# Early rows of an expert listed from 72 instead of 80 columns, their weights split on VectorE, later keys moved into the expert stage, five lists undeferred

## The chip, the cores and the metric

The kernel runs on one core of a Trainium2 chip. The metric is the device time of one execution in microseconds. One execution of each kernel was also profiled; times inside it are counted from the start of its span.

## The reference

Two layers follow each other. The first is a gated recurrence over 4 sequences of 5056 tokens with 256 channels; the second sends each of the 20224 rows to one of 8 experts with a capacity of 2528 rows each, by a greedy order over all (row, expert) logits, and runs that expert's two-layer network.

```
sig = 1 / (1 + exp(-f_logit)); f = lb + (1 - lb) * sig
for t in range(S): h = f[:, t] * h + (1 - f[:, t]) * x[:, t]; y[:, t] = h
logits = y.reshape(N, D) @ w_gate                 # N = 20224, D = 256, E = 8
for idx in argsort(-logits.flatten()):            # best pair first
    tok, e = idx // E, idx % E
    if assigned[tok] >= 0 or counts[e] >= N // E: continue
    assigned[tok] = e; counts[e] += 1
for e in range(E): out[assigned == e] = relu(y[assigned == e] @ w1[e]) @ w2[e]   # F = 1024
```

## The kernel before

Rows are held as 158 columns of 128 rows (a column is a tile of rows, NT = 158).

**Stage 1, the recurrence.** A loop over 40 chunks of four columns loads `x` and `f_logit` with SyncE's queue, takes the sigmoid on ScalarE, multiplies on GpSimd, transposes on TensorE, scans on VectorE (`g`) and transposes back with the logits beside the rows (`back`, PSUM `pr`, result `hr`). The rows go to a DRAM buffer `hbuf` from a ring of 22 buffers, half of them while the loop still loads and the rest behind it. `prep(c0, c1)` makes the keys of a block of columns in six steps: the best logit (`M`), its expert (`TMP`, `A`), an integer key (`K`), a one-hot table (`O`) and the first level of masks (`MK`). The loop does blocks of 32 columns as they become ready, and the last ones behind its end.

**Early rows.** When the keys of the first `CE` columns are there, `early` picks an expert that has at least `EARLY` first choices there (the fewest of those), loads its weights (`first_weights`, raw tiles `r`) and lists its first `EARLY` rows (`ids`), spread over the loop's iterations. `further` lists `MORE` rows from the remaining columns. These rows make a slot of their own, slot -1, of 14 tiles of 128 rows. `cut` notes which rows were taken (`EM`).

**Routing.** `route(r)` for r = 0 to 7 finds, round by round, the expert that fills first and the threshold of its last row. `search` does two halves of four levels: masks on VectorE (`MK`, two instructions of 80 columns), 20 small matmuls (`rt`), a masked sum (`DM`, `CR`), a matmul, a comparison (`FL`), a matmul and a new threshold (`TH`). At its end `GP` gives the result, then `assign`, `update`. `compact` writes the list of a slot, groups of two or three tiles at a time (`ids`), with sums on ScalarE (`junk`); a list starts only when the list ahead of it is done (`free`). For rounds below `AHEAD` the list of slot r follows round r at once; from `AHEAD` on a slot's list is made one round later (`pick`, `note`), so that the early rows' expert can be left to the last slot.

**Stage 2, the experts.** Slots -1 to 7 are worked through in chunks of up to four tiles, eight steps each. A step is `first` (six matmuls into `pw`, ScalarE writes `hh`, VectorE `hl`) and, three steps later, `second` (matmuls into `py` with both halves of `w2`). Operands are split into a high and a low part: `split` makes `w1h`, `w2s` on ScalarE and the low parts `w1l`, `w2s` on VectorE. For slot -1 two of the four low parts of w1 and all of w2 are made on GpSimd. Rows come by indirect DMAs of GpSimd (`gather`, tile `xg`) and are transposed (`trans`, `pt`, `xh`, `xl`).

**Order.** TensorE, VectorE and ScalarE run in the order in which the program issues. The program issues the expert steps and, at each `tick`, background generators: the routing (`main`), lists (`comp`) and weights (`sp`). A planner (`Pace`) with costs per instruction decides whether an engine would be free soon enough; `tick(True)` and `until` force a step whatever it says. When the gather of a slot's first chunk comes up, `ids_of` forces the routing and the list until its ids exist. While slot -1 runs, the routing pauses as long as slot 0 has fewer than eight tiles of ids. Before the first expert step the program forces a tick of the routing beside each piece of the first weights:

```
    sp = Bg(split(-1))
    main.tick(True)
    while not have(-1, "w1"):
        sp.tick(True)
        main.tick(True)
    trans(-1, 0, 0, True)
    main.tick(True)
    trans(-1, 0, 1, True)
```

Of the kernel before, what the change touches and what calls it, by code (L numbers as in the profile page):

```python
# [106 lines left out]
def kernel(ctx: ExitStack, tc: tile.TileContext, x: bass.AP, f_logit: bass.AP,  # L107
# [28 lines left out]
    CE, EARLY, MORE, AHEAD = 80, 1024, 768, 3  # L136
# [9 lines left out]
    PS, LASTC = 2, 152  # L146
# [190 lines left out]
    RSE = state.tile([P, CE + 2], BF, name="RSE")  # L337
    RAE = state.tile([P, CE + 2], BF, name="RAE")
    lv.tensor_copy(RSE[:, CE:CE + 1], pv)
    lv.tensor_copy(RSE[:, CE + 1:], pv)  # L340
# [198 lines left out]
    def blocks(ps, b0, n, w, at, ids):  # L539
        p3 = ps[:, :n * w].rearrange("p (b w) -> p b w", w=w)  # L540
        r = ohp.tile([P, 3, 4], F32, name="r")
        v.tensor_tensor(r[:, 0, :n], sq[:, b0:b0 + n], p3[:, :, w - 2], op=OP.subtract)
        v.tensor_scalar(r[:, 2, :n], p3[:, :, w - 1], float(at), None, op0=OP.add)
        yield
        for b in range(n):
            junk = ohp.tile([P, CE], F32, name="junk2")
# [3 lines left out]
        v.scalar_tensor_tensor(ids, r[:, 1, :n], float(P), r[:, 2, :n], op0=OP.mult, op1=OP.add)  # L550

    def ranks(c0, c1):
        em = EM[:, c0:c1]
        v.tensor_scalar(em, A1[:, c0:c1], ecode, 0.0, op0=OP.is_equal, op1=OP.add, accum_out=ecnt)
        v.tensor_tensor_scan(RSE[:, CE - c1 + c0:CE], onec[:, c0:c1], em, 0.0, op0=OP.mult, op1=OP.add)

    def offsets(ps, w):
        nc.tensor.matmul(ps[:, 160:161], tri, ecnt, start=True, stop=True)
        nc.tensor.matmul(ps[:, :w], nsub, RSE[:, CE + 2 - w:], start=True, stop=True)

    def steps_of(ps, w, rows):
        v.tensor_copy(RAE[:, :w], ps[:, :w])
        v.tensor_tensor(RAE[:, w - 2:w - 1], ecnt, RAE[:, w - 3:w - 2], op=OP.subtract)
        v.tensor_scalar(elim, ps[:, 160:161], -1.0, float(rows), op0=OP.mult, op1=OP.add)

    def cut(c0, c1):
        em = EM[:, c0:c1]
        v.scalar_tensor_tensor(em, RSE[:, CE - c1 + c0:CE], elim, em, op0=OP.is_le, op1=OP.mult)
        v.tensor_scalar(em, em, ecode, None, op0=OP.mult)

    def early(wi, ids):

        with nc.allow_low_precision(reason=EXACT):
            v.tensor_reduce(CR, O[:, :CE].rearrange("p c e -> p e c"), AX.X, OP.add)
        yield 'PE'
        ps = ppr.tile([P, 512], F32, name="pr")
        nc.tensor.matmul(ps[:, :E], ones_r, CR, start=True, stop=True)
        yield 'DVE'
        v.tensor_scalar(Q8, ps[:, :E], float(EARLY), 1.0e6, op0=OP.is_lt, op1=OP.mult)
        v.tensor_tensor(Q8, Q8, ps[:, :E], op=OP.add)  # L580
# [12 lines left out]
        g1 = {}  # L593
        st = ohp.tile([P, len(groups)], F32, name="st")

        def ge(k):
            g1[k] = ohp.tile([P, 512], BF, name="g1")
            v.tensor_scalar(g1[k], IO, st[:, k:k + 1], None, op0=OP.is_ge)
        v.tensor_scalar(st[:, 0:1], ps[:, 160:161], 0.0, None, op0=OP.add)
        v.tensor_scalar(st[:, 1:2], ps[:, 160:161], -512.0, None, op0=OP.add)  # L600
        steps_of(ps, w, EARLY)
        yield 'DVE'
        ge(0)
        for k in range(2):
            yield 'PE'
            ps = ppr.tile([P, 512], F32, name="pr")
            for b in range(4):
                nc.tensor.matmul(ps[:, b * w:(b + 1) * w], g1[k][:, b * P:(b + 1) * P], RAE, start=(b == 0),
                                 stop=(b == 3), skip_group_check=True)
            yield 'DVE'  # L610
            for n, _ in enumerate(blocks(ps, 4 * k, 4, w, 0, ids[:, 4 * k:4 * k + 4])):
                if n % 2:
                    yield 'DVE'
            if k == 0:
                yield 'DVE'
                ge(1)
        yield 'DVE'
        cut(0, CE)

    def further(rt, ids, prog):  # L620

        ranks(CE, NT)
        w = NT - CE + 2
        yield 'PE', RSE, ecnt
        ps = rt.tile([P, 512], F32, name="rt")
        offsets(ps, w)
        yield 'DVE', ps
        st = ohp.tile([P, len(groups)], F32, name="st")
        g1 = {}

        def ge(k):
            g1[k] = ohp.tile([P, 512], BF, name="g1")
            v.tensor_scalar(g1[k][:, :384], IO[:, :384], st[:, k:k + 1], None, op0=OP.is_ge)
        for k in range(2):
            v.tensor_scalar(st[:, k:k + 1], ps[:, 160:161], -384.0 * k, None, op0=OP.add)
        steps_of(ps, w, MORE)
        ge(0)
        for k in range(2):
            yield 'PE', RAE, g1[k]
            ps = rt.tile([P, 512], F32, name="rt")  # L640
            for b in range(3):
                nc.tensor.matmul(ps[:, b * w:(b + 1) * w], g1[k][:, b * P:(b + 1) * P], RAE[:, :w], start=(b == 0),
                                 stop=(b == 2), skip_group_check=True)
            yield 'DVE', ps
            if k == 0:
                ge(1)
            for _ in blocks(ps, 3 * k, 3, w, CE * P, ids[:, EARLY // P + 3 * k:EARLY // P + 3 * k + 3]):
                yield 'DVE',
            prog["ids"] = EARLY // P + 3 * k + 3
        cut(CE, NT)  # L650
        yield 'DVE',

# [73 lines left out]
    def prep(c0, c1):  # L726
# [3 lines left out]
        far = nc.vector if c1 > 128 else nc.gpsimd  # L730
# [46 lines left out]
    for i in range(NCH + 1):  # L777
# [7 lines left out]
        if i >= 1:  # L785
            back(i - 1)
            while stored < min(i - 1, int(SR * (i - 1)), CE // KT - 2):
                store(stored)
                stored += 1
        if i >= 4:  # L790
            build(2)
        upto = chunks[i - 1][0] // 8 * 8 if i else 0
        upto = NC if i == NCH else min(upto, LASTC)
        if upto - done >= 32 or upto > done and upto in (CE, LASTC, NC):
            preps.append(prep(done, upto))
            done = upto
        prep_step(99 if i == NCH else (3 if upto == CE else 1 if est is not None else PS) if upto < LASTC else 5)
        if due == 'PE':
            next(est)
        elif est is None and done >= CE and not preps:  # L800
            est = early(WIE, IDE)
    for _ in est:
        pass
# [94 lines left out]
def moe(ctx, tc, g):  # L898
# [8 lines left out]
    tri, cM, IO, RA, sq, ident = (g[k] for k in ("tri", "cM", "IO", "RA", "sq", "ident"))  # L907
# [19 lines left out]
    def layout(k):  # L927
        ns = {-1: [4, 4, 4, 2], E - 1: [4, 2]}.get(k, [4] * 5)
# [43 lines left out]
    def split(k):  # L972
# [61 lines left out]
    posts, step = [], 0  # L1034
# [63 lines left out]
    def second(k, c, j):  # L1098
# [3 lines left out]
        for q, n in enumerate(ns):  # L1102
# [17 lines left out]
            elif j == FB - 1 and q % 2 == 1:  # L1120
                turn = (len(SC) + sum(what[0] == "s" for what, _ in issues)) // 2
                issue(upto=lambda what: what[0] == "s" and what[1] <= turn - YB)
                y = yp.tile([P, 2, D], F32, name="y")
                m = min(ns[q - 1:q + 1])
                if m == P:
                    nc.scalar.activation(y, PY[q // 2], AF.Copy)
                else:
                    nc.scalar.activation(y[:, 0], PY[q // 2][:, 0], AF.Copy)
                    nc.scalar.activation(y[:n, 1], py, AF.Copy)
                issues.extend((("s", turn), store(k, c, r, ns[r], y)) for r in (q - 1, q))  # L1130
# [37 lines left out]
    def all_routes():  # L1168
# [3 lines left out]
        def slot(k):  # L1172
# [8 lines left out]
            return WI[k], spawn  # L1181
        for r in range(E):
            yield from route(r, rt, slot, free)

# [14 lines left out]
    comp[-1] = Bg(further(rc, IDS[-1], prog[-1]))  # L1199
    gather(*order[0])  # L1200
    issue(4)
    sp = Bg(split(-1))
    main.tick(True)
    while not have(-1, "w1"):
        sp.tick(True)
        main.tick(True)
    trans(-1, 0, 0, True)
    main.tick(True)
    trans(-1, 0, 1, True)
    gather(*gathers.pop(0))  # L1210
    issue(4)
    while not sp.done:
        sp.tick(True)
        main.tick(True)
    sp = None
# [4 lines left out]
    def tick():  # L1220
# [9 lines left out]
        if sp is None:  # L1230
# [134 lines left out]
```

## Time and profile before

| what | value |
|---|---|
| median of 3 runs | 1226.45 us (1224.43 to 1227.23) |
| the profiled execution's own time | 1225.41 us |
| its span | 1223.5 us |
| TensorE matmul busy | 1157.2 us, 95% |
| VectorE busy | 810.8 us, 66% |
| ScalarE busy | 538.2 us, 44% |
| GpSimd busy | 473.6 us, 39% |
| mean granted TensorE clock | 0.977 |

PE is TensorE's matmuls, PEld its weight loads, DVE VectorE, ACT ScalarE, POOL GpSimd, SP SyncE. PEclk is the granted TensorE clock as a share of its full speed. Matmuls overlap, so busy time of TensorE is not its peak rate. The chain from the recurrence to the expert stage is the part of the profile around 160 to 200 us; the eight large slots follow from about 288 us.

### The profile page before, as it was taken

What the parts mean: (1) busy time and instruction counts of PE and PEld (TensorE: products, weight loads), DVE (VectorE), ACT (ScalarE), POOL (GpSimd) and SP (SyncE); (2) the same over time, 40 slices, a digit from 0 to 9 for tenths busy, and PEclk for the clock granted to TensorE, in tenths of its full rate; (3) what the DMA queues carried; (4) which work ended last, traced back from release to release, by engine and by line L of the source; (5) the groups of instructions that cost most, each with busy time, mean ns of one, the idle gap of its engine ahead of it and who ended that gap; (6) DMA issues with size and microseconds to landing.
All of it is one profiled execution on the core that took longest, in us unless ns stands there. A gap on an engine that the chain in (4) does not pass through costs nothing.

```text
span 1223.5 us, 22589 instructions
## 1 busy us (share of the span) xinstructions
PE 1157.2 (95%) x8821; PEld 1050.9 (86%) x8821; DVE 810.8 (66%) x1945; ACT 538.2 (44%) x1088; POOL 473.6 (39%) x468
## 2 busy tenths in 40 slices
PE   7999767999999999999996899999999999999997
PEld 7898756889889888999895788889899899999996
DVE  6999897678778767778777678867644542252221
ACT  7887662254335425342223434443544642352332
POOL 6666672333334333333222244234333333433322
PEclk9999987999999999999997999999999999999999
DMA  9998994121131113111102113013111311211100
GB/s 357 352 337 301 342 337 140 40 100 53 45 103 54 45 47 104 48 41 40 43 27 92 36 48 108 31 44 122 44 45 52 109 44 48 98 63 48 43 31 31
DMA packets 52447, 125.25 MB, mean 102 GB/s; under 512 B 8062, under 2 KB 28288, under 8 KB 51184
## 3 DMA queue, kind: packets, MB, share of 16 engines
q0 software_dynamic: 19248, 60.96, 15.0%
q1 hardware_dynamic: 32544, 62.78, 14.8%
q8 instruction: 71, 1.16, 0.4%
q14 instruction: 40, 0.33, 0.1%
q10 hardware_dynamic: 544, 0.01, 0.0%
HBM read 81.69 MB, written 42.10 MB: 101 GB/s over the span
## 4 chain that ended last, share of the span: by engine, by line
PE 56%; issue 19%; POOL 9%; DVE 3%; ACT 1%; DMA 1%; POOLq 0%; ACTq 0%; DVEq 0%
PE py L100 25%; PE pw L100 24%; POOL out_dram L100 4%; POOL xg L100 4%; PE rt L100 3%; PE pt L100 1%; PE pr L100 1%; DMA xg<-hbuf,ids 1%; POOL r L100 1%; DVE MK L100 1%; DVE TMP L100 0%; PE pf L100 0%; PE pb L100 0%; ACT w1h L100 0%; DVE K L100 0%
## 5 line engine op out<-in xcount | busy, mean ns | idle before, releaser
L100 PE MATMUL py<-w2s,hh 128*128 128x256 f32 x2560 | 492.9, 289 | 0.5 <-ACT y L100 0.5
L100 ACT ACTIVATE hh<-pw 128x512 fp32r<-128x512 f32 (+2 forms) x328 | 190.8, 582 | 536.5 <-PE pw L100 461.6
L100 PEld LDWEIGHTS py<-w2s,hh 128*128 128x128 f32 x2560 | 409.7, 190 | 16.8 <-ACT y L100 0.7
L100 DVE SCALAR_TENSOR_TENSOR hl<-pw,hh 128x512 fp32r<-128x512 f32 (+2 forms) x328 | 219.7, 670 | 244.6 <-ACT hh L100 243.9
L100 PE MATMUL py<-w2s,hl 128*128 128x256 f32 (+1 forms) x1280 | 363.1, 284 | 0.0
L100 POOL DMA_INDIRECT out_dram<-y,ids x160 | 165.2, 1033 | 337.5 <-ACT hh L100 271.4
L100 POOL DMA_INDIRECT xg<-hbuf,ids x160 | 163.3, 1021 | 298.7 <-ACT hh L100 237.9
L100 PE MATMUL pw<-xh,w1h 128*128 128x512 f32 (+2 forms) x656 | 259.0, 395 | 0.0
L100 PE MATMUL pw<-xl,w1h 128*128 128x512 f32 (+2 forms) x656 | 258.2, 394 | 0.0
L100 PE MATMUL pw<-xh,w1l 128*128 128x512 f32 (+2 forms) x656 | 256.0, 390 | 0.0
L100 PEld LDWEIGHTS py<-w2s,hl 128*128 128x128 f32 (+1 forms) x1280 | 243.7, 190 | 0.0
L100 PEld LDWEIGHTS pw<-xh,w1l 128*128 128x128 f32 x656 | 125.0, 191 | 23.5
L100 PEld LDWEIGHTS pw<-xh,w1h 128*128 128x128 f32 x656 | 126.0, 192 | 12.6
L100 PEld LDWEIGHTS pw<-xl,w1h 128*128 128x128 f32 x656 | 126.0, 192 | 12.0
L100 POOL TENSOR_TENSOR xl<-fl,xl 128x1024 f32<-128x1024 f32 (+2 forms) x40 | 92.9, 2323 | 46.4 <-ACT fl L100 33.6
L100 DVE TENSOR_TENSOR_SCAN g<-fg,g,pb 128x512 f32<-128x512 f32 (+4 forms) x78 | 92.8, 1228 | 8.7 <-ACT fg L100 4.3
L100 PE MATMUL pr<-iw,g 128*128 128x136 f32 x632 | 81.8, 281 | 4.0 <-DVE hr L100 3.4
L100 PEld LDWEIGHTS pr<-iw,g 128*128 128x128 f32 x632 | 76.8, 191 | 5.3 <-DVE hr L100 4.0
L100 ACT ACTIVATE junk<-rt,r 128x158 bf16<-128x158 f32 x146 | 57.2, 392 | 37.6 <-DVE r L100 33.2
L100 ACT ACTIVATE fg<-pf,one,nomlb 128x512 f32<-128x512 f32 (+1 forms) x80 | 57.5, 767 | 8.7 <-PE pf L100 6.9
L100 PE MATMUL rt<-O,MK 128*128 128x64 bf16 x1120 | 43.7, 195 | 14.9 <-DVE MK L100 14.9
L100 DVE TENSOR_TENSOR xl<-pt,xh 128x512 fp32r<-128x512 f32 (+1 forms) x80 | 54.1, 676 | 3.8 <-ACT xh L100 3.6
(217 smaller groups left out, 1212.5 us busy)
## 6 DMA issues: line engine op xcount, KB each, us to landing
hbuf<-hr SPq DMA_DIRECT2D x39, 528.0 KB, 8.8
fl<-in_f_logit_dram SPq DMA_DIRECT2D x38, 512.0 KB, 6.2
xl<-in_x_dram SPq DMA_DIRECT2D x38, 512.0 KB, 6.6
xg<-hbuf,ids POOLq DMA_INDIRECT x160, 2.8
out_dram<-y,ids POOLq DMA_INDIRECT x160, 2.4
fl<-in_f_logit_dram SPq DMA_DIRECT2D x3, 256.0 KB, 4.4
xl<-in_x_dram SPq DMA_DIRECT2D x3, 256.0 KB, 4.6
r<-in_moe_w_dram,wi POOLq DMA_INDIRECT x27, 6.0
```

What stands on the lines that cost most here:

```text
L100: r = f(*args, **kw)
```

## The change

`CE`, `EARLY`, `MORE` and `AHEAD` take new values: the early list covers 896 rows out of 72 columns, the further one 1024 rows out of 86. Slot -1 then has 15 tiles in chunks of 4, 3, 4 and 4, and the last slot 5 (3 and 2) instead of 6. Five slots get their list right after their round. The keys of columns 72 to 103 are made in the loop after the early list is done; those of columns 104 to 157 are made by `further`, in the expert stage, and the routing waits for them (`all`). The further list is summed on ScalarE (`act`) instead of VectorE, and each of the lists has its own number of tiles per group. The low parts of the first weights are all made on VectorE, of which three ahead of the first expert matmul and the rest at the first ticks. A chunk of three tiles stores its last tile alone.

```
-    CE, EARLY, MORE, AHEAD = 80, 1024, 768, 3
+    CE, EARLY, MORE, AHEAD = 72, 896, 1024, 5
...
-    PS, LASTC = 2, 152
+    PS, RW = 2, NT - CE
...
-    def blocks(ps, b0, n, w, at, ids):
+    def blocks(ps, b0, n, w, at, ids, act):
...
+        if act:
+            v.tensor_scalar(r[:, 2, :n], p3[:, :, w - 1], float(at + (w - 2) * P // 2), None, op0=OP.add)
+            yield 'ACT', r
+            for b in range(n):
+                junk = ohp.tile([P, NT], BF, name="junk")
+                nc.scalar.activation(junk[:, :w - 2], p3[:, b, :w - 2], AF.Sign, bias=r[:, 0, b:b + 1], scale=-1.0,
+                                     accum_out=r[:, 1, b:b + 1])
+            yield 'DVE', r
+            v.scalar_tensor_tensor(ids, r[:, 1, :n], float(P // 2), r[:, 2, :n], op0=OP.mult, op1=OP.add)
+            return
...
     def further(rt, ids, prog):
+
+        cut(0, CE)
+        yield 'DVE',
+        for c in range(104, NT, 32):
+            for _ in prep(c, min(c + 32, NC)):
+                yield 'DVE',
+        prog["all"] = True
         ranks(CE, NT)
...
-        for k in range(2):
+        at = EARLY // P
+        for k, n in enumerate((4, MORE // P - 4)):
...
-        far = nc.vector if c1 > 128 else nc.gpsimd
+        far = v if c0 >= CE else nc.gpsimd
...
-        upto = chunks[i - 1][0] // 8 * 8 if i else 0
-        upto = NC if i == NCH else min(upto, LASTC)
-        if upto - done >= 32 or upto > done and upto in (CE, LASTC, NC):
+        upto = min(chunks[i - 1][0] // 8 * 8, CE) if i else 0
+        if upto - done >= 32 or upto > done and upto == CE:
             preps.append(prep(done, upto))
             done = upto
-        prep_step(99 if i == NCH else (3 if upto == CE else 1 if est is not None else PS) if upto < LASTC else 5)
+        if est is not None and due is None and not preps and done < 104:
+            preps.append(prep(CE, 104))
+            done = 104
+        prep_step(3 if upto == CE and done == CE else 1 if done > CE else PS)
...
-        ns = {-1: [4, 4, 4, 2], E - 1: [4, 2]}.get(k, [4] * 5)
+        ns = {-1: [4, 3, 4, 4], E - 1: [3, 2]}.get(k, [4] * 5)
...
-            if k < 0 and i == 5:
+            if k < 0 and i == 3:
                 prog[k]["w1"] = 1
...
-                    (nc.gpsimd if k < 0 else v).tensor_sub(lo, src, hi.bitcast(F32))
-                elif k < 0 and i in (2, 4):
-                    nc.gpsimd.tensor_scalar(src, src, scale, None, op0=OP.mult)
-                    nc.gpsimd.tensor_sub(lo, src, hi.bitcast(F32))
+                    v.tensor_sub(lo, src, hi.bitcast(F32))
...
+        while not prog[-1].get("all"):
+            yield 'DVE',
         for r in range(E):
             yield from route(r, rt, slot, free)
+            if r == 0:
+                cut(CE, NT)
...
     sp = Bg(split(-1))
-    main.tick(True)
     while not have(-1, "w1"):
         sp.tick(True)
-        main.tick(True)
     trans(-1, 0, 0, True)
-    main.tick(True)
     trans(-1, 0, 1, True)
     gather(*gathers.pop(0))
-    issue(4)
-    while not sp.done:
-        sp.tick(True)
-        main.tick(True)
-    sp = None
+    issue(3)
...
-        if sp is None:
+        if k < 0 and wn == 0 and sp is not None:
+            sp.tick(True)
+            if sp.done:
+                sp = None
+        elif sp is None:
```

## Rows read from the trace of the kernel before

**Rows 1.** Windows: us, busy us and count by engine, PEclk, DMA share, GB/s
```profile
140.00:160.00 20.00, 16.35 (x144) 15.76 (x143) 18.47 (x33) 13.98 (x25) 11.46 (x9) 1.00 0.89 280
171.20:194.73 23.53, 4.53 (x50) 3.48 (x47) 21.59 (x36) 5.35 (x10) 19.49 (x16) 0.55 1.08 352
194.73:286.68 91.95, 89.97 (x697) 80.01 (x697) 66.86 (x192) 35.67 (x74) 27.66 (x27) 0.97 0.19 61
...
412.80:540.32 127.52, 127.52 (x1030) 114.14 (x1026) 92.34 (x250) 53.51 (x125) 43.05 (x43) 1.00 0.18 59
540.32:683.76 143.44, 132.07 (x1037) 118.44 (x1038) 110.78 (x288) 43.23 (x80) 41.92 (x39) 0.95 0.15 49
683.76:822.79 139.03, 133.34 (x1078) 118.51 (x1077) 102.06 (x291) 56.81 (x134) 48.82 (x44) 0.98 0.17 55
...
1061.92:1177.56 115.64, 115.64 (x762) 105.48 (x761) 40.37 (x58) 41.40 (x69) 40.05 (x41) 1.00 0.19 62
```
**Rows 2.** Timeline of TensorE: start, us, instruction, [idle before and releaser]
```profile
185.15 0.16 PE L100 MATMUL rt<-FL,eighth 128*128 128x1 bf16 x1 [0.75 <-DVE FL L100]
185.18 0.73 PE L100 MATMUL pt<-identr,xg 128*128 128x128 f32 x4
...
194.73 0.77 PE L100 MATMUL pw<-xh,w1h 128*128 128x512 f32 x1
```
**Rows 3.** Timeline of VectorE ahead of the first expert matmul
```profile
182.41 1.13 DVE L100 SCALAR_TENSOR_TENSOR w1l<-r,omlb,w1h 128x512 fp32r<-128x512 f32 x1
...
185.68 0.83 DVE L100 TENSOR_TENSOR MK<-K,TH 128x1280 bf16<-128x1280 int16 x1
186.57 0.69 DVE L100 TENSOR_TENSOR xl<-pt,xh 128x512 fp32r<-128x512 f32 x1
187.18 5.88 DVE L100 TENSOR_TENSOR MK<-K,TH 128x1280 bf16<-128x1280 int16 x1
```
**Rows 4.** Timeline of GpSimd in the same stretch
```profile
172.57 1.03 POOL L100 DMA_INDIRECT xg<-hbuf,ids  x1 [0.51 <-issue]
...
187.44 4.92 POOL L100 TENSOR_TENSOR w2s<-r,w2s 128x512 fp32r<-128x512 f32 x4
```
**Rows 5.** Windows of the search's matmuls alone (tile rt) in slots 1 to 3
```profile
412.80:540.32 127.52, 15.25 (x269) 1.00 0.18 59
540.32:683.76 143.44, 15.26 (x275) 0.95 0.15 49
683.76:822.79 139.03, 17.05 (x316) 0.98 0.17 55
```
**Rows 6.** Timeline of VectorE: a masked sum, results of rounds (GP), ids of lists
```profile
193.93 0.22 DVE L100 TENSOR_TENSOR DM<-rt,bm 128x64 f32<-128x64 f32 x1
...
245.27 0.28 DVE L100 TENSOR_TENSOR GP<-rt,rE 128x120 f32<-128x120 f32 x1 [0.94 <-ACT CN L100]
...
264.73 0.15 DVE L100 SCALAR_TENSOR_TENSOR ids<-r 128x2 int32<-128x2 f32 x1
...
369.33 0.16 DVE L100 SCALAR_TENSOR_TENSOR ids<-r 128x2 int32<-128x2 f32 x1 [0.20 <-ACT junk L100]
...
567.47 0.28 DVE L100 TENSOR_TENSOR GP<-rt,rE 128x120 f32<-128x120 f32 x1 [0.96 <-ACT CN L100]
...
644.59 0.28 DVE L100 TENSOR_TENSOR GP<-rt,rE 128x120 f32<-128x120 f32 x1 [0.90 <-ACT CN L100]
```
**Rows 7.** DMA issues from 150 to 200 us: count, median us to landing
```profile
xg<-hbuf,ids POOLq DMA_INDIRECT x8, 6.1
```
**Rows 8.** Timeline of VectorE: first and last of a key block's eight instructions
```profile
163.64 0.41 DVE L100 TENSOR_REDUCE M<-X 128x32 f32<-128x256 f32 x1
...
170.80 0.74 DVE L100 TENSOR_TENSOR MK<-K,thr0f 128x512 bf16<-128x512 int16 x1
```
**Rows 9.** The page's list of DMA issues over the whole span
```profile
xg<-hbuf,ids POOLq DMA_INDIRECT x160, 2.8
```
**Rows 10.** Timeline of GpSimd during slot 0
```profile
372.79 1.81 POOL L100 DMA_INDIRECT xg<-hbuf,ids  x1 [0.30 <-issue]
```

More of the change, by code (lines that the diff above doesn't have):

```diff
@@ L336 @@
     EM = state.tile([P, NC], F32, name="EM")
[L337 to L340, printed above, removed]
+    RSE = state.tile([P, RW + 2], BF, name="RSE")
+    RAE = state.tile([P, RW + 2], BF, name="RAE")
+    lv.tensor_copy(RSE[:, RW:RW + 1], pv)
+    lv.tensor_copy(RSE[:, RW + 1:], pv)
     nc.gpsimd.memset(EM[:, NT:], 0.0)
@@ L542, in blocks @@
         v.tensor_tensor(r[:, 0, :n], sq[:, b0:b0 + n], p3[:, :, w - 2], op=OP.subtract)
-        v.tensor_scalar(r[:, 2, :n], p3[:, :, w - 1], float(at), None, op0=OP.add)
+        if act:
[8 more added lines that the diff above has]
+            return
         yield
         for b in range(n):
-            junk = ohp.tile([P, CE], F32, name="junk2")
+            junk = ohp.tile([P, RW], F32, name="junk2")
             v.tensor_scalar(junk[:, :w - 2], p3[:, b, :w - 2], r[:, 0, b:b + 1], 0.0, op0=OP.is_le, op1=OP.add,
@@ L549, in blocks @@
             yield
-        v.scalar_tensor_tensor(ids, r[:, 1, :n], float(P), r[:, 2, :n], op0=OP.mult, op1=OP.add)
+        v.scalar_tensor_tensor(ids, r[:, 1, :n], float(P), p3[:, :, w - 1], op0=OP.mult, op1=OP.add)
     def ranks(c0, c1):
@@ L603, in early, with further @@
         ge(0)
-        for k in range(2):
+        for k, n in enumerate((4, EARLY // P - 4)):
             yield 'PE'
             ps = ppr.tile([P, 512], F32, name="pr")
-            for b in range(4):
-                nc.tensor.matmul(ps[:, b * w:(b + 1) * w], g1[k][:, b * P:(b + 1) * P], RAE, start=(b == 0),
-                                 stop=(b == 3), skip_group_check=True)
+            for b in range(n):
+                nc.tensor.matmul(ps[:, b * w:(b + 1) * w], g1[k][:, b * P:(b + 1) * P], RAE[:, :w], start=(b == 0),
+                                 stop=(b == n - 1), skip_group_check=True)
             yield 'DVE'
-            for n, _ in enumerate(blocks(ps, 4 * k, 4, w, 0, ids[:, 4 * k:4 * k + 4])):
-                if n % 2:
+            if k == 0:
+                ge(1)
+            for m, _ in enumerate(blocks(ps, 4 * k, n, w, 0, ids[:, 4 * k:4 * k + n], False)):
+                if m % 2 == 0:
                     yield 'DVE'
[L614 to L617, printed above, removed]
+    def further(rt, ids, prog):
         cut(0, CE)
-    def further(rt, ids, prog):
+        yield 'DVE',
[3 more added lines that the diff above has]
+        prog["all"] = True
         ranks(CE, NT)
@@ L646, in further @@
                 ge(1)
[L647 to L651, printed above, removed]
+            yield from blocks(ps, 4 * k, n, w, CE * P, ids[:, at:at + n], True)
+            at += n
+            prog["ids"] = at
     def update(rt, first):
@@ L786 @@
             back(i - 1)
-            while stored < min(i - 1, int(SR * (i - 1)), CE // KT - 2):
+            while stored < min(i - 1, int(SR * (i - 1)), 18):
                 store(stored)
@@ L801 @@
             est = early(WIE, IDE)
+    prep_step(99)
     for _ in est:
@@ L905, in moe @@
                        "ROWS", "w1v", "w2v", "CE", "EARLY"))
-    tri, cM, IO, RA, sq, ident = (g[k] for k in ("tri", "cM", "IO", "RA", "sq", "ident"))
+    tri, cM, IO, RA, sq, ident, cut, NC = (g[k] for k in ("tri", "cM", "IO", "RA", "sq", "ident", "cut", "NC"))
     def pool(name, bufs, **kw):
@@ L1032, in ready @@
             return (self.up is None or self.up.done) and pace.due(self.eng, self.tiles, 1e9)
-    posts, step = [], 0
+    posts, step, pairs = [], 0, [0]
     def post(eng, tiles, emit, up=None, now=False):
@@ L1119, in second @@
                 issue(99)
-            elif j == FB - 1 and q % 2 == 1:
-                turn = (len(SC) + sum(what[0] == "s" for what, _ in issues)) // 2
+            elif j == FB - 1 and (q % 2 == 1 or q == len(ns) - 1):
+                turn = pairs[0] = pairs[0] + 1
                 issue(upto=lambda what: what[0] == "s" and what[1] <= turn - YB)
                 y = yp.tile([P, 2, D], F32, name="y")
-                m = min(ns[q - 1:q + 1])
-                if m == P:
+                rows = range(q - q % 2, q + 1)
+                if len(rows) == 2 and min(ns[r] for r in rows) == P:
                     nc.scalar.activation(y, PY[q // 2], AF.Copy)
                 else:
-                    nc.scalar.activation(y[:, 0], PY[q // 2][:, 0], AF.Copy)
-                    nc.scalar.activation(y[:n, 1], py, AF.Copy)
-                issues.extend((("s", turn), store(k, c, r, ns[r], y)) for r in (q - 1, q))
+                    for r in rows:
+                        nc.scalar.activation(y[:ns[r], r % 2], PY[q // 2][:ns[r], r % 2], AF.Copy)
+                issues.extend((("s", turn), store(k, c, r, ns[r], y)) for r in rows)
     class Bg:
@@ L1199, in moe @@
     comp[-1] = Bg(further(rc, IDS[-1], prog[-1]))
+    prog[-1]["ids"] = EARLY // P
     gather(*order[0])
```

17 lines of the change are left out of this document (8 added, 9 removed).

## The prediction

> **What bounds the kernel now.** I read the page first (busy shares, the 40 slices), then the windows by stage, then the timelines of each engine where TensorE is not full. The reader should see in the windows that TensorE is the bound of the expert stage: in the stretch of slot 6 it is busy 115.64 of 115.64 us [rows 1]. So a tile costs 115.64 / 20 = 5.78 us there, a step of four tiles 4 x 5.78 / 8 = 2.9 us. Work of other engines costs nothing there as long as TensorE does not wait. TensorE has two holes that matter.
>
> The first lies between the end of the recurrence and the first expert matmul. From 171.2 to 194.73 it is busy 4.53 of 23.53 us, VectorE 21.59 [rows 1]. TensorE waits for masks and sums of VectorE, and the transposes of the first rows, which need only the gathers, stand behind the search's matmul of 185.15 in its queue [rows 2]. VectorE itself is held up: the same mask operation takes 0.83 us at 185.68 and 5.88 at 187.18, and in that second stretch GpSimd runs the four subtractions of the weights, 4.92 us from 187.44 [rows 3, 4].
>
> The second hole is in slots 2 and 3. Slots 1 and 2 carry the same matmuls of the search, 15.25 and 15.26 us [rows 5], but slot 1 takes 127.52 us with no idle time and slot 2 takes 143.44 with 11.37 idle, the rest being a clock of 0.95. Slot 3 takes 139.03, with 17.05 of search [rows 1, 5]. The code says why: slot 3 takes its list only after round 4, whose result comes at 644.59, and the emitter then forces the rest of that round and of the list with no expert matmuls between. Round 3's result was there at 567.47 [rows 6].
>
> **The change part by part.** *Start of the expert stage.* The search's first level, the keys of columns 104 to 157 and four subtractions of weights no longer stand before the first expert matmul. What stays: the fourth gather starts at 172.57 [rows 4] and lands after 6.1 us while the stores drain [rows 7], at 178.7. Then transposes 0.73 [rows 2], a copy on ScalarE (taken like VectorE's subtraction, 0.69 [rows 3]), the subtraction 0.69, and the second half's transposes 0.73: first matmul at about 181.5, 13.2 earlier. The three low parts of w1 that it needs are 3 x 1.13 = 3.4 us on VectorE [rows 3], hidden while the gathers land. If that cover went they would cost up to 3.4.
>
> *Recurrence.* VectorE loses the keys of 54 columns. A block of 32 takes eight instructions, 3.2 us [rows 8], so 54 take 5.4; the list and the estimate use 72 instead of 80 columns, which I count as nothing because each instruction is mostly fixed cost. From 140 to 160 VectorE is busy 18.47 of 20 us and TensorE 16.35 [rows 1]: at most 3.65 us can come back, at least none (the input loads may be the limit). I take 1.5, since both engines have other partners to wait for. Together the stage starts at 180.0, 14.7 earlier.
>
> *First steps on VectorE.* The last low part of w1 (1.13), four of w2 (nearest row the subtraction of xl, 0.69 each), cut (two small instructions, taken as 0.5) and the keys (5.4) are 9.8 us that now stand among the first steps' hl. Weights are forced one per tick, keys only when VectorE is at most 2 us ahead in the planner. Nothing waited here before in this form: cost between 0 (VectorE has 2.2 us free per step) and 5 (all forced pieces, 1.13 + 2.8, before the first hl, and one hl late). I take 2, because TensorE itself starts at the low clock (0.55 in the stretch before [rows 1]).
>
> *Search of round 0 while TensorE is full.* Two batches of 20 mask matmuls that lay in the hole are now in its queue. The search costs 15.25 us in slot 1 for 269 instructions [rows 5], so 40 matmuls and their companions 2.3 at most, 1.2 taken.
>
> *Slot 0.* Before, round 0 stood at its second reduction (193.93) when the stage began, its result came at 245.27, its first four tiles of ids at 264.73 [rows 6]. Counted from the stage's start at 194.73: 50.5 and 70.0 us. Now the keys come first: four steps, about 12 us; then the first level (1) and the second, which I take as a usual one, 8 (51.3 us for six and a half levels [rows 6]). So the result at 12 + 1 + 8 + 51.3 = 72, the ids at 72 + 19.5 = 91.5. Then four gathers at 1.0 each plus landing 2.8 [rows 4, 9] and 2.8 of transposing: 9.6 if forced, so slot 0 can start 101 after the stage's start. Fourteen tiles took 91.95 [rows 1]; fifteen take 97.7. Three halves of steps (3 x 1.45 = 4.3 us) are then still in hand to cover the wait. That would leave nothing, but the weights of slot 0 and pacing of gathers (one per 2.9-us step, 11.6 for four) come on top: 0 to 8, and I take 4, plus 1.5 for a clock that falls as it did in slot 2. 5.5 in all.
>
> *Five lists undeferred.* Slot 3's list now follows round 3 (567.47, then the start of a list as in round 0, 19.5 us, stretched to 50 beside a search) against a need near 645. Slot 4's follows round 4 in the same way. Slot 2 then should cost what slot 1 does, 127.5 instead of 143.44, gain 15.9; slot 3 127.5 + (17.05 - 15.25) = 129.3 instead of 139.03, gain 9.7 [rows 1, 5]. 25.6 together. If the lists come late again, 0.
>
> *Tiles.* 15 early ones and 5 in the last slot instead of 14 and 6: 160 as before, six chunks as before. Nothing. Blocks of the further list on ScalarE instead of VectorE: ScalarE is busy 35.67 of 91.95 us there [rows 1], nothing.
>
> Sum: 1223.5 - 14.7 + 2 + 1.2 + 5.5 - 25.6 = 1191.9 of span. The profiled time is 1.9 above its span, so 1193.8; the median of the three runs stands 1.0 above that execution: 1194.8. I say 1194.5.
>
> **A rule weighed.** Once, one gather took 1.81 us on GpSimd (372.79), with VectorE writing a step matrix and a low part of weights beside it, against 1.03 at 172.57 [rows 4, 10]. The Trainium skill (SBUF — State Buffer, "SBUF: two separate sides") says that VectorE and GpSimd share a port pair that one instruction holds to its end, so that a DMA issued by GpSimd waits for its descriptors while VectorE runs in a two-port mode; it speaks against putting the weights on VectorE just when the gathers are issued; the one long row agrees, the other does not, though VectorE was no less busy there. By the rule the sum is that of rival C, by the usual row it is mine.
>
> **The rivals.** (A) *Slot 0 waits longer.* Keys and masks get fewer turns than I count, the result comes 85 after the start: 13 more, 1207.5. For: VectorE was over 90% busy in the hole. Against: it is busy 66.86 of 91.95 in the early stage [rows 1]. (B) *The first tiles or gathers wait for the row stores*, whose buffers lie under the expert stage's tiles. Before, the transposes ran at 185.18 and nothing but VectorE held what followed, so at the latest the stage starts at 185.2 + 0.73 + 0.69 + 0.69 + 0.73 = 188: 8 more, 1202.5. For: the DMA engines are full (share 1.08 [rows 1]). Against: no row shows such a wait [rows 2]. (C) *Each of the four first gathers is stretched as the one row was*, 4 x 0.78 = 3.1: 1197.6. (D) *The search falls behind later.* Round 0 ends 21 us later after the start, slot 0 starts only about 11 later, so rounds lose 10 us against the slots. Slot 1's first four ids were there at 369.33, its first result left at 412.8 [rows 1, 6]: 43 us, of which 22 are needed at an unhurried pace. A hole like slot 2's elsewhere is 15.9: 1210. (E) *Undeferring does not do what it says*, since a list cannot start before the list ahead of it is done: 1220. (F) *Slower.* Round 0 is held behind the keys (the gate "all"), and TensorE eats the 15 tiles first. Each us that the result comes after about 68 costs one; it must come at 104, the keys done 44 after the start instead of 12, to take back the 31.7. For: the gate exists. Against: 9.8 us of work beside 25 us of free VectorE time.
>
> **How the numbers follow.** Forecast 0.40, A 0.17, B 0.14, C 0.06, D 0.12, E 0.06, F 0.05. The likeliest gives 1194.5. Below it: the full 3.65 instead of 1.5 in the recurrence, no waits at the start and at slot 0 is 2.2 + 2 + 5.5 less, 1185, and the 1.98 us for which TensorE was idle in the early stage (91.95 - 89.97 [rows 1]) may go too: low 1182. Above: A, B, C and D lie up to 1210, E and F are left out (0.11): high 1212. 0.2% is 2.5 us, about what a measurement of this kernel can tell from no change. Faster is everything but F and the part of E near no gain: 0.93; same 0.02; slower 0.05.
>
> **What would show it.** Right: first expert matmul near 180; no tensor operations on GpSimd there, masks under 0.9 us; round 0's result some 72 us after the start and a gap of a few us ahead of slot 0; slots 2 and 3 near 127 and 129 us with TensorE full. Wrong: first matmul at 188 or later with a wait for a store (B); a gap over 12 us ahead of slot 0 (A); new gaps ahead of slots 1 or 5 (D); a gap ahead of slot 3 unchanged (E).

## The result and the profile after

The changed kernel takes 1211.21 us (median of four runs, 1210.67 to 1213.59) where the kernel before takes 1226.28: a ratio of 0.9883, interval 0.9865 to 0.9901. That is 15 us faster. The forecast was 1194.5, 32 us faster, so half of the gain is missing. The profiled execution has a span of 1208.9 us (1210.67 in all).

Windows of the changed kernel by stage (us, busy us and count by engine, PEclk, DMA share, GB/s): a piece of the recurrence, its end to the first expert matmul, slot -1, slots 1, 2, 3 and 6.

```profile
140.00:160.00 20.00, 18.91 (x169) 18.70 (x167) 16.59 (x26) 16.92 (x30) 12.39 (x11) 1.00 0.96 292
171.46:188.69 17.23, 2.02 (x10) 1.28 (x9) 3.19 (x6) 2.59 (x5) 5.97 (x8) 0.55 1.08 355
188.69:300.43 111.74, 100.07 (x751) 89.06 (x750) 77.78 (x219) 41.92 (x97) 26.24 (x25) 0.93 0.22 70
430.53:557.97 127.44, 127.44 (x1030) 114.04 (x1026) 92.34 (x250) 53.56 (x124) 42.97 (x43) 1.00 0.19 59
557.97:686.11 128.14, 128.14 (x1051) 115.27 (x1052) 103.83 (x291) 50.53 (x112) 47.68 (x43) 1.00 0.19 59
686.11:813.77 127.66, 127.66 (x1048) 114.75 (x1047) 103.60 (x274) 50.36 (x110) 45.84 (x43) 1.00 0.19 59
1053.48:1168.64 115.16, 115.16 (x760) 105.23 (x759) 40.09 (x58) 41.22 (x69) 39.10 (x40) 1.00 0.19 61
```

Against [rows 1]: slots 2 and 3 are full and take 128.14 and 127.66 us instead of 143.44 and 139.03, which is 26.7 gained where 25.6 was forecast. The stage starts at 188.69 instead of 194.73: 6.0 gained of 14.7. In the 17.23 us ahead of it every engine is idle most of the time, VectorE too (3.19 us busy), while the DMA engines are full (share 1.08); before, VectorE was busy nearly all of that stretch. Slot -1, up to slot 0's first matmul, takes 111.74 us for 15 tiles where 97.7 and 8.7 of delays had been forecast.

What the engines wait for there is seen in their timelines (start, us, instruction, [idle before and releaser]): TensorE, VectorE, ScalarE and GpSimd of the changed kernel.

```profile
179.56 0.37 PE L100 MATMUL pt<-identr,xg 128*128 128x128 f32 x1 [1.12 <-DMA xg<-hbuf,ids]
188.14 0.75 PE L100 MATMUL pt<-identr,xg 128*128 128x128 f32 x4 [8.21 <-DVE xl L100]
199.99 0.50 PE L100 MATMUL pw<-xh,w1h 128*128 128x512 f32 x1 [4.67 <-DVE hl L100]
...
187.39 0.69 DVE L100 TENSOR_TENSOR xl<-pt,xh 128x512 fp32r<-128x512 f32 x1 [13.44 <-DMA hbuf<-hr]
199.25 0.69 DVE L100 SCALAR_TENSOR_TENSOR hl<-pw,hh 128x512 fp32r<-128x512 f32 x1 [4.44 <-DMA hbuf<-hr]
...
179.97 0.60 ACT L100 ACTIVATE xh<-pt 128x512 fp32r<-128x512 f32 x1 [6.51 <-PE pt L100]
196.87 1.08 ACT L100 ACTIVATE hh<-pw 128x512 fp32r<-128x512 f32 x2 [4.66 <-DMA hbuf<-hr]
...
182.27 0.10 POOL L100 MEMSET gap<- 128x1 f32 x1 [3.55 <-DMA hbuf<-hr]
```

The last of the first four gathers has landed when its transpose runs at 179.56, and `xh` is copied at 179.97, both as forecast. Then VectorE, whose idle time of 13.44 us ends at 187.39, can't write `xl` before a store of rows to `hbuf` has landed. TensorE stands 8.21 us. A second time, `hh` and `hl` wait for such stores, and TensorE stands 4.67 us more. The chain of work that ended last shows the second of these waits too: the last store, issued at 190.40, and behind it `hl` (start us, us, what).

```profile
190.40 8.72 DMA hbuf<-hr
...
199.25 0.70 DVE hl L100
```

Neither `xl` nor `hl` reads `hbuf`. They wait for memory. The allocation of the changed kernel puts the expert stage's tiles over the ring of 22 row buffers (bytes within a partition; in the last column the chunks of rows whose buffers lie there last):

```
tile        bytes             last chunks in the ring buffers there
w2s (wa2)   192576 .. 208960  23, 24, 25, and a gate buffer
gap         184384 .. 192576  27, 28
xl, first   122944 .. 127040  29, 31
hh, first   131136 .. 133184  33
hh, second  139328 .. 141376  37
hl, first   141376 .. 143424  37, 39
```

SyncE issues the last stores in the order of the chunks, 17 to 39, between 154.63 and 192.30, one each 1.64 us. So each wait can be laid beside the landing of the last store that reads the tile's memory (us, rounded):

```
tile        chunk  store issued  to landing  landed  wait ended
gap         28     171.1         11.1        182.2   182.27
xl, first   31     176.1         11.2        187.3   187.39
hh, second  37     187.4          9.3        196.8   196.87
hl, first   39     190.4          8.7        199.1   199.25
```

Each wait ends within 0.2 us behind that landing.

Around the start of slot 0 (300.43) there are four small waits of TensorE, three ahead of it (5.6 us) and one behind it, 6.3 us together:

```profile
276.40 0.31 PE L100 MATMUL rt<-RA,g 128*128 128x160 bf16 x2 [2.08 <-DVE RA L100]
...
293.82 0.36 PE L100 MATMUL pt<-identr,xg 128*128 128x128 f32 x2 [0.52 <-DMA xg<-hbuf,ids]
297.19 0.75 PE L100 MATMUL pt<-identr,xg 128*128 128x128 f32 x4 [3.00 <-DVE xl L100]
...
312.43 0.28 PE L100 MATMUL pt<-identr,xg 128*128 128x128 f32 x1 [0.69 <-DMA xg<-hbuf,ids]
```

### The profile page after: what moved, and what is told of

Read it like the earlier page. It is cut to its first block, busy times and chain, and to the rows that moved or that the text cites. A ratio compares the mean times of both kernels' runs of the same rounds, so it can differ in the third digit from the quotient of the medians.

```text
span 1208.9 us, 22553 instructions
## 1 busy us (share of the span) xinstructions
PE 1153.3 (95%) x8821; PEld 1048.4 (87%) x8821; DVE 793.4 (66%) x1917; ACT 539.0 (45%) x1104; POOL 461.3 (38%) x459
## 4 chain that ended last, share of the span: by engine, by line
PE 80%; DMA 3%; issue 3%; DVE 1%; POOL 1%; ACT 0%; POOLq 0%; DVEq 0%; SPq 0%; ACTq 0%
PE py L100 37%; PE pw L100 35%; PE rt L100 4%; PE pt L100 2%; DMA hbuf<-hr 1%; PE pr L100 1%; DMA xg<-hbuf,ids 1%; DMA r<-in_moe_w_dram,wi 1%; PE pf L100 1%; PE pb L100 0%; POOL xg L100 0%; POOL out_dram L100 0%; DVE g L100 0%; ACT hh L100 0%; DVE hl L100 0%
## 5 line engine op out<-in xcount | busy, mean ns | idle before, releaser
L100 ACT ACTIVATE hh<-pw 128x512 fp32r<-128x512 f32 (+3 forms) x328 | 191.2, 583 | 553.1 <-PE pw L100 470.8
L100 DVE SCALAR_TENSOR_TENSOR hl<-pw,hh 128x512 fp32r<-128x512 f32 (+3 forms) x328 | 219.6, 670 | 232.8 <-ACT hh L100 228.0
L100 PE MATMUL pw<-xh,w1h 128*128 128x512 f32 (+3 forms) x656 | 258.3, 394 | 4.7 <-DVE hl L100 4.7
L100 PE MATMUL pw<-xl,w1h 128*128 128x512 f32 (+3 forms) x656 | 259.1, 395 | 0.0
L100 PE MATMUL pw<-xh,w1l 128*128 128x512 f32 (+3 forms) x656 | 256.3, 391 | 0.0
L100 ACT ACTIVATE junk<-rt,r 128x158 bf16<-128x158 f32 (+1 forms) x153 | 59.4, 389 | 17.3 <-DVE r L100 14.4
L100 DVE TENSOR_TENSOR xl<-pt,xh 128x512 fp32r<-128x512 f32 (+2 forms) x81 | 54.2, 670 | 16.9 <-DMA hbuf<-hr 13.4
L100 PEld LDWEIGHTS pt<-identr,xg 128*128 128x128 f32 x320 | 36.4, 141 | 31.6 <-DVE xl L100 11.5
```

Of the source, the lines that this page charges most:

```text
L100: r = f(*args, **kw)
```

## The experiments

**Theory and rivals.** The theory: the start of the stage and the first `hh` and `hl` wait for the drain of the row stores, and for that alone; moving these tiles to memory that comes free earlier gives back the 8.7 us at the start, the 4.67 us after it, and some of the lower clock (0.93 in slot -1). The rivals: the first steps are held by VectorE or the gathers as well, so that other waits take their place; or the parts of the change depend on each other, and the early rows and the five lists can't be priced apart.

**e1: only `xh` and `xl` moved.** A filler keeps their old place, and they are allocated last, over buffers of the recurrence.

```
-    xp = pool("xp", 2)
+    gap2 = pool("gap2", 1)
+    gap2_t = gap2.tile([P, 4096], F32, name="gap2")
     hp = pool("hp", 5)
...
     wa2 = pool("wa2", 1)
+    xp = pool("xp", 2)
```

> The changed kernel with one edit: the pool of the transposed rows (xh, xl) is allocated last, over what the forget gates and products of the recurrence used, so that it no longer lies over ring buffers that are stored late; the pool of hh and hl stays where it was. Theory (the first tiles of the expert stage wait until the row stores that read the same memory have landed): xl follows xh at once, the first expert matmul moves from 188.69 to 181 to 182.5 us; but hh and hl still lie over ring buffers stored last (their waits ended at 196.87 and 199.25), TensorE runs its three pw buffers and stands there, now for 11 to 13 us instead of 4.67, and the kernel is 0 to 2 us faster (1209 to 1211). Rival (xl waits for something else, the VectorE or the landing of rows): the first expert matmul stays at 188 to 189. Second rival (hh and hl were late only because the stage started late and would come earlier): the stage keeps most of the 7 us, 1203 to 1205.

Measured: 1212.02 us, 0.9889 (0.9873 to 0.9906) of before; the changed kernel had 0.9883. Its TensorE, ScalarE and VectorE:

```profile
181.72 0.75 PE L100 MATMUL pt<-identr,xg 128*128 128x128 f32 x4 [1.41 <-DVE xl L100]
199.85 0.80 PE L100 MATMUL pw<-xh,w1h 128*128 128x512 f32 x1 [10.86 <-DVE hl L100]
...
190.23 0.60 ACT L100 ACTIVATE hh<-pw 128x512 fp32r<-128x512 f32 x1 [5.05 <-DMA hbuf<-hr]
196.68 1.08 ACT L100 ACTIVATE hh<-pw 128x512 fp32r<-128x512 f32 x2 [5.86 <-DMA hbuf<-hr]
...
199.10 0.69 DVE L100 SCALAR_TENSOR_TENSOR hl<-pw,hh 128x512 fp32r<-128x512 f32 x1 [10.70 <-DMA hbuf<-hr]
```

As the theory had it: the first wait falls from 8.21 us to 1.41, what it was in the kernel before, the second grows from 4.67 to 10.86 us and ends at the same time (199.85, against 199.99), and nothing is gained. Both rivals fall: `xl` waited for nothing else that comes later, and an earlier start doesn't bring `hh` and `hl` earlier, since the dates are those of the stores.

**e2: `hh` and `hl` moved too.** `xh` and `xl` lie over the four ring buffers stored first in the drain, `hh` and `hl` over buffers of the recurrence, slot 0's weights and the `y` tiles, which are needed later, over those stored last.

```
     wa1 = pool("wa1", 1)
     YB = 3
+    wb_ = pool("wb", 1)
+    gap1 = pool("gap1", 1)
+    gap1_t = gap1.tile([P, 1184], F32, name="gap1")
+    xp = pool("xp", 2)
     yp = pool("yp", YB)
-    xp = pool("xp", 2)
+    gap = pool("gap", 1)
+    gap_t = gap.tile([P, 5056], F32, name="gap")
+    wa2 = pool("wa2", 1)
     hp = pool("hp", 5)
-    wb_ = pool("wb", 1)
-    gap = pool("gap", 1)
-    gap_t = gap.tile([P, 2048], F32, name="gap")
-    nc.gpsimd.memset(gap_t[:, :1], 0.0)
-    wa2 = pool("wa2", 1)
```

> The changed kernel with the pools in another order: the transposed rows (xh, xl) over the four ring buffers that are stored first in the drain, hh and hl over the forget gates and products of the recurrence, slot 0's weights and the y tiles over the ring buffers stored last; the gap tile is larger and is not written. No instruction changes but that one memset of one column falls away. Theory: first expert matmul at 181 to 182.5 us instead of 188.69, and no wait of hh or hl for a store (4.67 us on TensorE in the changed kernel): with up to 2 us of lower clock that goes with the gap, 11 to 14 us faster than the changed kernel, 1197 to 1200 us. Rival (the stage's first steps are held by VectorE and by gathers as well): start at 181 to 182.5, but other gaps appear in the first 25 us, and 3 to 8 us are gained, 1203 to 1208.

Measured: 1200.78 us, 0.979 (0.9773 to 0.9806) of before, 10 to 11 us faster than the changed kernel. Windows of e2 from the end of the recurrence to the first expert matmul, and of slot -1:

```profile
174.55:185.13 10.58, 1.93 (x10) 1.24 (x9) 3.19 (x6) 2.59 (x5) 5.90 (x7) 0.72 1.08 361
185.13:289.35 104.22, 96.94 (x751) 86.15 (x751) 77.47 (x219) 42.04 (x97) 26.46 (x25) 0.96 0.31 97
```

Its TensorE at the start of the stage:

```profile
182.80 0.37 PE L100 MATMUL pt<-identr,xg 128*128 128x128 f32 x1 [1.23 <-DMA xg<-hbuf,ids]
184.58 0.75 PE L100 MATMUL pt<-identr,xg 128*128 128x128 f32 x4 [1.41 <-DVE xl L100]
191.88 0.50 PE L100 MATMUL pw<-xh,w1h 128*128 128x512 f32 x1 [0.38 <-DVE hl L100]
```

The recurrence of this execution ended at 174.55, 3.1 later than in the changed kernel's, though its code is the same. In the ten profiles of kernels with the changed loop that end lies between 171.5 and 174.7, in the four with the loop of before between 170.2 and 171.2. So stages are compared from it. End of recurrence to first matmul: 17.23 us in the changed kernel, 10.58 here. Slot -1: 111.74 and 104.22. Of these 7.5, 4.3 are the wait for `hl` (4.67 there, 0.38 here), and 3.1 go with the clock, 0.93 there and 0.96 here: TensorE is busy 100.07 and 96.94 us with the same 751 matmuls. Together 14.2; the span shows 9.8, with the 3.1 of the recurrence and 1.3 elsewhere between them. The first matmul, at 185.13, missed the 181 to 182.5 expected by no more than that 3.1. The gain of 11 to 14 expected was just missed in the time (10.4) and holds for the span from the recurrence's end on (1208.9 - 171.46 against 1199.1 - 174.55, 12.9 less). No other wait took the place of those removed.

**e3 and e4: the five lists alone, and all but them.** One number each, `AHEAD` 3 to 5 in the kernel before, and 5 to 3 in the changed one.

> The kernel before with one number of the change alone: five lists are assigned in their own round instead of three (AHEAD 3 to 5). Theory (the parts of the change are independent; slots 2 and 3, 143.44 and 139.03 us long before, become full slots of 127.5 to 128): 26 to 27 us faster than before, 1199 to 1201 us, so that it is faster than the changed kernel by about 11. Rival (the undeferred rounds need the other parts: without them the lists of slots 3 and 4 come late): the slots 2 to 5 show gaps and the gain is 5 to 20, 1206 to 1221 us.

> The changed kernel with three lists undeferred as before (AHEAD 5 to 3), all else of the change kept. Theory: slots 2 and 3 are long again (143 and 139 us), the kernel takes 26 to 27 us more than the changed one, 1237 to 1239 us: the early part of the change by itself is 11 to 12 us slower than the kernel before. Rival (the changed early stage lets the search run ahead, and slots 2 and 3 wait less even so): 1220 to 1232 us.

Measured: e3 1199.72 us, 0.9788 (0.9771 to 0.9804); e4 1237.56 us, 1.0101 (1.0085 to 1.0118). Windows of slots 2 and 3 in e3:

```profile
540.53:668.70 128.17, 128.17 (x1051) 115.30 (x1052) 103.78 (x291) 50.59 (x112) 47.57 (x43) 1.00 0.18 59
668.70:796.38 127.68, 127.68 (x1048) 114.74 (x1047) 103.57 (x274) 50.24 (x111) 45.80 (x43) 1.00 0.18 59
```

and in e4:

```profile
556.33:701.85 145.52, 132.74 (x1037) 118.88 (x1038) 110.67 (x288) 43.29 (x79) 42.61 (x39) 0.94 0.15 48
701.85:840.78 138.93, 133.32 (x1078) 118.29 (x1077) 102.14 (x291) 56.70 (x134) 48.73 (x44) 0.98 0.17 55
```

The parts add up. Undeferring is worth 25.9 us on the kernel before (1225.60 in these runs) and 26.4 on the changed one, and everything else of the change, by itself, makes the kernel 12 us slower. One number of the diff gives more than the whole diff.

**e8: the pools of e2 in the kernel before with five lists.** It asks whether the stores cost anything before the change.

> The kernel before with five lists undeferred (e3) and with the pools in the order of e2. Theory (before the change VectorE's masks and the search of round 0 held the stage until 194.73 us, when most row stores had landed, so that the memory under xl, hh and hl cost nothing): within 2 us of e3, 1198 to 1201 us. Rival (the stores held something there too): 3 us or more below e3.

Measured: 0.9782 (0.9755 to 0.9809) of before (1204.93 us; the kernel before took 1231.36 in these runs, so ratios are compared from here on). e3 had 0.9788: nothing gained that these intervals show. The wait for the stores was covered, and the change uncovered it.

**e5 and e6: one early tile more, one fewer.** In e2, with 16 tiles (`EARLY` 1024, chunks of 4, 4, 4, 4 and 2, 2) and with 14 (`MORE` 896, chunks of 4, 3, 4, 3 and 4, 2).

> The kernel of e2 (changed kernel, pools in the other order) with 16 early tiles instead of 15: 1024 rows out of the estimate on 72 columns instead of 896, 1024 further rows as before; slot 7 has 4 tiles instead of 5, so that the number of tiles stays. In e2 TensorE still stands ahead of slot 0 for round 0's search and first list: 2.06 us for RA, 0.52 for rows, 2.99 for xl, 0.73 for rows. Theory (round 0 is too late for 15 tiles): one more tile, some 6.5 us of work, covers most of these 6.3 us: 4 to 7 us faster than e2, 1194 to 1197 us. Rival (the waits move with the work, since the list is asked for only when it is due): within 1.5 us of e2, 1199 to 1202.

> The kernel of e2 with 14 early tiles instead of 15 (896 further rows instead of 1024; slot 7 has 6 tiles). Theory (round 0's search sets the start of slot 0): the work ahead of it is 6.5 us shorter, the search is not, so TensorE waits 5 to 7 us longer there: 1206 to 1208 us. Rival (the waits move with the work): within 1.5 us of e2.

Measured: e5 0.976 (0.9733 to 0.9788), e6 0.9848 (0.982 to 0.9875), against 0.979 of e2. As ratios times 1225.6 that is 4 us less and 7 us more, near the theory for both, but the interval of e5 reaches e2. So both were run side by side.

**e9 to e12, on one chip.** e2 again, 16 tiles again, 16 tiles with a second PSUM buffer for the forced transposes, and e3 again.

```
-        pt = tps.tile([P, 512], F32R, name="pt").rearrange(
+        pt = (pws.tile([P, 512], F32R, name="pw") if now and h
+              else tps.tile([P, 512], F32R, name="pt")).rearrange(
```

> The kernel of e2 (changed kernel, pools in the other order) again, beside the next three on one chip. Theory: ratio 0.977 to 0.981 to the kernel before, as in e2.

> The kernel of e5 (e2 with 16 early tiles) again, on the chip of e9. Theory (round 0's list sets the start of slot 0, and one tile more covers part of it): 3 to 6 us below e9. Rival (e5 and e2 differ by their chips alone): within 1.5 us of e9.

> The kernel of e5 with one edit: where the transposes of a chunk are forced (at the start of the stage and of slot 0), the second half goes to a PSUM buffer of the first products (pw) instead of waiting for the one pt buffer, which VectorE frees with xl. In e5 TensorE waits 1.41 us for xl at the start of the stage and 2.99 us ahead of slot 0. Theory: the second half runs while xh of the first half is written, so 1.0 to 1.4 us fall away at each of the two places: 2 to 3 us below e10. Rival (the first matmuls wait for the xl of the first half just as long): within 1 us of e10.

> The kernel of e3 (the kernel before with five lists undeferred and nothing else of the change) again, on the chip of e9 to e11. Theory (with the stores out of its way the early part of the change is worth nothing at 15 tiles, and something at 16): within 2 us of e9, and 3 to 6 us above e10. Rival: e9 is below it by 3 us or more.

```
e9   15 tiles, pools moved            1203.57 us   0.9769 (0.9756 to 0.9783)
e10  16 tiles, pools moved            1203.71      0.9771 (0.9758 to 0.9785)
e11  16 tiles, second buffer          1201.14      0.9754 (0.9739 to 0.9769)
e12  kernel before, five lists        1204.61      0.9779 (0.9765 to 0.9792)
```

The rival of e10 came true in the time: 16 tiles gain nothing in the median. The windows show a gain and where it was lost. Slot -1 up to slot 0's first matmul in e6, 14 tiles:

```profile
184.03:288.41 104.38, 97.50 (x760) 88.71 (x759) 74.43 (x213) 40.71 (x95) 28.09 (x26) 0.94 0.31 99
```

The same in e9, 15 tiles, and under it the recurrence from 10 us on:

```profile
182.01:289.26 107.25, 100.10 (x750) 88.97 (x750) 77.45 (x218) 41.98 (x97) 25.75 (x25) 0.93 0.30 94
10.00:171.63 161.63, 147.47 (x1265) 143.03 (x1263) 143.52 (x244) 129.50 (x216) 107.88 (x86) 0.99 0.97 338
```

Both in e10, 16 tiles:

```profile
184.41:294.35 109.94, 103.37 (x777) 89.46 (x777) 79.41 (x219) 43.69 (x97) 27.34 (x26) 0.97 0.31 97
10.00:174.68 164.68, 149.49 (x1267) 145.49 (x1265) 142.86 (x245) 129.53 (x216) 107.64 (x86) 0.99 0.95 331
```

A tile is 5.8 us of work [rows 1]. From e9 to e10, on one chip, the stage grows by 2.7 us for one tile more, and from e6 to e5, on another, by 5.5 us for two (e5 took 109.91). So about half of each added tile was cover. (e2, the kernel of e9, took 104.22, so a single such difference can be off by 3 us.) In e6 all 336 of slot -1's sums (`py`) stand ahead of slot 0's first matmul, in e9 324 of 360. With 14 tiles all of that work is thus done there, and TensorE still stands 5.6 us for round 0's list (3.55 for `RA`, 2.01 for `xl`): round 0's search and list set the start of slot 0. That wait is no longer than e2's 5.6, against e6's theory; the time came true because the sums filled it and because slots 0 and 2 took 1.4 and 2.9 us more than in e9 (130.53 and 132.17). But the recurrence of e10 ended 3.05 later than that of e9. Whether that is the eighth block of the list, which is made in the recurrence, or the spread seen above, is not settled: the kernels with 16 tiles ended it at 174.35, 174.68 and 173.07, that with 14 at 173.68, those with 15 at 171.46 to 174.55.

e11 has the lowest median, but its interval overlaps those of e9 and e10. Its edit took effect at the start only, where the first matmul comes 8.86 us after the recurrence instead of 9.73; ahead of slot 0 the wait of 2.96 us for `xl` stayed, since there the transposes are not issued as forced ones and still share one buffer. Of the 2 to 3 us expected the windows show 0.9. e12 is within an interval of e9, as expected, but not the 3 to 6 us above e10 that were expected too: it is 0.9 above. Without the stores in its way the early part of the change is worth nothing that these intervals show; only its loss is gone.

**e7: low halves of the weights on GpSimd again,** in e2.

```
-                    v.tensor_sub(lo, src, hi.bitcast(F32))
+                    (nc.gpsimd if k < 0 else v).tensor_sub(lo, src, hi.bitcast(F32))
+                elif k < 0 and i in (2, 4):
+                    nc.gpsimd.tensor_scalar(src, src, scale, None, op0=OP.mult)
+                    nc.gpsimd.tensor_sub(lo, src, hi.bitcast(F32))
```

> The kernel of e2 with the split of slot -1's weights as before: the low halves of two pieces of w1 (multiply and subtract) and of the four of w2 on GpSimd instead of VectorE. Theory (the GpSimd pieces are long, 4.92 us for one of w2 in the trace before, and stretch VectorE's operations beside them, as 5.88 us instead of 0.83 for MK there): the first expert matmul or the first sums of w2 wait 6 to 15 us, 1206 to 1216 us. Rival (the pieces are due late enough and VectorE gains the time that it saves): within 2 us of e2, 1199 to 1203.

Measured: 0.9783 (0.9754 to 0.9812), as e2: the rival. GpSimd and VectorE of e7:

```profile
183.78 2.60 POOL L100 TENSOR_SCALAR r<-r,omlb 128x512 f32<-128x512 f32 x1
187.97 5.62 POOL L100 TENSOR_TENSOR w2s<-r,w2s 128x512 fp32r<-128x512 f32 x4
...
185.12 1.32 DVE L100 TENSOR_SCALAR EM<-EM,esc 128x72 f32<-128x72 f32 x1
186.48 1.81 DVE L100 TENSOR_TENSOR TMP<-X,M 128x256 f32<-128x256 f32 x1
192.36 1.77 DVE L100 TENSOR_TENSOR MK<-K,thr0f 128x512 bf16<-128x512 int16 x1
```

The four pieces of `w2` take 5.62 us together, not 4.92 each: the row [rows 4] stands for four instructions (its x4), and I had read it as one in this expectation. VectorE's operations beside GpSimd's are stretched, `TMP` from 0.42 to 1.81 us and `MK` from 0.68 to 1.77 (e2 and e7), and TensorE waits 2.63 us for `hl` once. But round 0's result comes 66.1 us after the first matmul (248.91), where it comes after 68.6 in e2 and 70.3 in e9, which can make up for it. Moving the split to VectorE was worth nothing that these intervals show.

## Why the prediction was wrong, point by point

**Start of the expert stage.** This is the step that failed. The chain of durations was right as far as it went: gathers landed and `xh` copied near 180, as forecast. It left out that `xl` must own its memory, a wait that it put at nothing. The stage started 8.7 us later than forecast; 6.8 of that is this wait (8.21 us, of which 1.41 stay in e1), the rest the recurrence below. The forecast had the same gap a second time behind the start, 4.67 us for `hl`. Rival B named just this, put the stage's start at 188 at the latest (188.69 came; chunk 31's store landed at 187.3, in the kernel before at 184.7) and gave it 0.14, on the ground that "no row shows such a wait". That ground was false. I had read TensorE's timeline [rows 2], and the wait stood on ScalarE's, in the kernel before:

```profile
174.52 1.15 ACT L100 ACTIVATE w2s<-r 128x512 fp32r<-128x512 f32 x2 [1.35 <-DMA hbuf<-hr]
```

`w2s` lies over chunk 25's buffer there too. The row shows both the kind of wait and its date, 174.52 for chunk 25, from which the other 14 follow at 1.64 us each, to 197.5 for the last. Rival B was too cheap as well, 8 us, since it saw the start and not the `hl` behind it.

**First steps on VectorE.** Forecast +2, for pieces of weights ahead of the first `hl`. Measured: TensorE waited 4.67 us for `hl`, but VectorE was idle for 4.44 of that, waiting for the last store. In e2, with the same work on VectorE and no stores, the wait is 0.38 us. So the term itself was near nothing and another wait stood in its place.

**Recurrence.** Forecast -1.5; its last matmul ends at 171.46 instead of 171.17, 0.3 later. VectorE is busy 16.59 us from 140 to 160 instead of 18.47 [rows 1], so the work did go, and nothing came back. Over all profiles the term has the wrong sign: the changed loop ended at 173.0 in the mean of ten, the loop of before at 170.9 in the mean of four, and each of the ten lies behind each of the four. What costs these 2 us no run shows.

**Search of round 0, and slot 0.** Forecast: 97.7 for 15 tiles, 2, 1.2 and 5.5, together 106.4. Measured without the stores: 104.22 (e2) and 107.25 (e9). The three waits ahead of slot 0 are 5.6 us in the changed kernel, and e6 shows that they are round 0's. Round 0's result came 76.2 us after the start (264.86 - 188.69) with the 4.67 us stall, 68.6 in e2, for 72 forecast. Rival A did not happen.

**Five lists undeferred.** 26.7 for 25.6 forecast, shown alone by e3 and e4. Slot 1 and slots 4 to 7 have no new gap: rivals D and E did not happen.

**The rule weighed.** The first four gathers took 1.08, 1.67, 1.08 and 1.15 us on GpSimd, 0.9 us more than the four before, not the 3.1 of rival C, and the last landed as forecast. The trace agrees with the rule (the Trainium skill, SBUF — State Buffer, "SBUF: two separate sides") in direction, here and in e7's stretched operations on VectorE; but neither cost any time that these runs show. The forecast's ground against it was misread: beside the short row of 172.57 VectorE was not as busy, it ran nothing from 172.08 to 173.20.

**The sum.** Missing 17.0 us of span (1208.9 against 1191.9). The start gives 8.7, slot -1 5.3 (111.74 against 106.4), slots 2 and 3 give back 1.1. The remaining 4 are in slot 0 (128.51 us from its first matmul to slot 1's first, 124.53 before). The last chunk ahead of it has four tiles instead of two, so 36 of slot -1's sums fall behind the boundary instead of 18, and the stretch holds 67.24 us of `py` work against 65.11; 0.69 is the wait for rows at 312.43. In e2 the start, from the recurrence's end, and slot -1 are 14.2 shorter.

**Why the early part is worth nothing even then.** In e3 the stretch from the recurrence's end to the first expert matmul is 23.55 us long, in e2 10.58: 13 us. But the search and keys that filled it are now in slot -1, whose TensorE waits for round 0 all the same: 104.22 us against 92.22, 12 more for one tile of 5.8. The tile comes back in the last slot (39.6 us from its first matmul to the last one in e3, 34.1 in e2), and slot 0 takes 4.3 more than in e3, some 2 of them at the boundary above. Of the 13 some 2 are left, and the recurrence ends some 2 later. The search's time was moved, not saved.

## What to carry to other kernels

When a stage is to start earlier, ask of each tile it writes first what lay in that memory before and when the last reader, a DMA too, lets go; the order of pools is part of the schedule. Look for the first sign of such a wait on every engine's timeline, not only on the bound engine's: a wait of 1.35 us on an idle engine gave the date of a drain that cost 13 us. And try the parts of a change alone: here one number gave all of the gain.

## What had not been expected

With one wait removed the next wait, on the same drain, took its whole place (e1: 10.86 us instead of 8.21 and 4.67, the end 0.14 apart): two waits for one date cost what the later one costs. And one profile is a weak witness for a gain of 3 us. With the same loop the recurrence ended up to 3.2 us apart (171.5 to 174.7), and e2 and e9, the same kernel on two chips, differ by 5.8 us behind it (1024.6 and 1030.3); the kernel before took 1225.6 and 1231.5 us there. Such a gain is better read side by side, stage by stage, on one chip.
